# Feed-forward buffers of a whole chunk, two linear steps once per chunk, the first chunk in halves and a new order, in a linear-attention and rational feed-forward kernel

## The chip, the cores and the metric

The kernel runs on one core of one Trainium2 chip. The metric is the device time of one execution in microseconds (us). Five runs of the kernel before gave 249.75, 250.07, 250.63, 252.65 and 254.08 us, a median of 250.63 us.

## What is computed

Two stages follow each other. The first is attention without a softmax: keys and queries (4 batches, 4 heads, 1,088 tokens, 32 numbers each) are turned into 64 features, the outer product of two projections to 8 numbers each. The second is a feed-forward layer whose activation is a quotient of two polynomials. Cut to what matters:

```python
phi(x) = outer(S1 x, S2 x)                      # 8 * 8 = 64 features
kv  = sum over tokens of phi(k) v ; z = sum of phi(k)
x   = (phi(q) kv) / (phi(q) z + 1e-6)           # 4352 tokens x 128
h   = x @ w_in                                  # 128 -> 2048
P   = a0 + a1*h + a2*h^2 + a3*h^3
Q   = 1 + |b0|*|h| + |b1|*h^2
out = (P / (Q + 1e-6)) @ w_out                  # 2048 -> 128
```

## The kernel before, in words

**Tiling.** 4,096 of the 4,352 tokens are worked in eight *chunks* of 512 tokens (two per batch, n = 0 to 7). The 64 last tokens of each batch make a ninth chunk of 256 tokens, the remainder. The 2,048 hidden units are 16 blocks of 128, so the hidden layer of a chunk is a matrix of 128 partitions by 16 x 512 = 8,192 columns. It is worked in *groups* of blocks (`add_group`, L561): the first chunk in groups of 4, 4 and 8 blocks (`FIRST`, L20), each other chunk in two groups of 8 blocks, which is 4,096 columns, and the remainder in 8, 4 and 4 (`LAST`, L21). Groups are numbered g0 to g19 through the whole kernel: g0 to g2 are chunk 0, g3 and g4 chunk 1, g15 and g16 chunk 7, g17 to g19 the remainder.

**A group.** TensorE makes two blocks at a time into PSUM (L572). ScalarE (a few times VectorE) copies them to SBUF as bf16, `hb` (L578, the copy itself in the helper at L184 or L186). Inputs are scaled ahead so that |b0| and |b1| fall out of the formula. VectorE then makes, each one instruction over the whole group:

- `s` = h*h (step `sq`, L582) and `u` = |h| by clearing the sign bit (`ab`, L585)
- `t` = a3*h + a2 (`hi`, L603), `t` = t*s (`cu`, L607), and in place `hb` = a1*h + a0 (`lo`, L610)
- at the end `t` = t*u (`ov`, L621)

Two sums stand between them: `u` = u + s (step `us`) and `t` = t + hb (step `ts`). `add_sum` (L596) gives each of them either to a DMA that accumulates from SBUF into SBUF and is issued by GpSimd (POOL, L594), or to VectorE (L592). ScalarE turns `u` into 1/Q as exp(-ln(..)): `ln` (L614) and `ex` (L618), 4,096 columns at most each. `project` (step `pj`, L629) multiplies `t` by w_out into one PSUM tile for the chunk, which is copied (`eT`) and stored.

**The attention steps.** Per chunk of keys: transposes (L383), projection (L392), copy of one half (`ea`), outer product (`pd`, L403), sum over tokens (L421). Per chunk of queries: transposes (L487), copy (`ev`), expansion by two matmuls (L499), copy of one to `A_sb`, product (`pd`, L506), numerator and denominator (L519), division (`dv`, L526 to L529), transposes of the result (L535) and a copy with a scale to `xT` (`xe`, L540 or L542). With `xT` the matmuls of the hidden layer can begin.

**What sets the order.** Each step is added to a plan with its engine, and `ORDER` (L46) is a list, written out, in which the steps are issued. Each engine carries out its own steps strictly in that order, so a step that waits holds up everything behind it on its engine, DMA issues included. `ENGINE` (L28) names the steps that do not go to their usual engine. `BUFS` (L25) gives the number of buffers: four of one group each for `hb`, `u` and `t`, two for `s`. A tile that takes over a buffer waits until every reader and writer of the tile before it is done. `HOME` (L38) says which PSUM pool small steps use. `fill` steps (L742) are matmuls on zeros; `SKIP` names those left out.

Of the kernel before, what the change touches and what calls it, by code (L numbers as in the profile page):

```python
# [19 lines left out]
FIRST = [4, 4, 8]  # L20
LAST = [8, 4, 4]  # L21
LW = 4096
FILLS = 16

BUFS = dict(xT=3, hb=4, s=2, u=4, t=4, k_sb=2, v=1, q=2, L=1, h_ps=3, out_ps=1, w_ps=1,  # L25
# [3 lines left out]
    "ld.S0": "ACT", "ld.S1": "ACT", "ld.a": "ACT", "ld.b": "ACT", "k00.ea": "DVE", "k01.ea": "DVE", "kr.ev": "DVE",  # L29
    "kr.ea": "DVE", "k0.s0": "DVE", "q1.ev": "DVE", "q2.ev": "DVE", "k20.ea": "DVE", "q5.xe": "DVE", "k30.ea": "DVE",  # L30
    "k31.ea": "DVE", "q7.ev": "DVE", "q8.xe": "DVE", "g1.ts": "DVE", "o0.eT": "DVE", "o1.eT": "DVE", "g7.e4": "DVE",
    "o3.eT": "DVE", "o5.eT": "DVE", "g13.e4": "DVE", "g17.us": "DVE", "g18.ts": "DVE", "o8.eT": "DVE",
}

FOUR = []
SKIP = ["f3"]

HOME = {  # L38
    "k00.T": "h_ps", "k00.ab": "h_ps", "k01.T": "h_ps", "k01.ab": "h_ps", "kv.0": "h_ps", "q0.T": "h_ps",
    "q0.xT": "h_ps", "q1.T": "h_ps", "k11.T": "h_ps", "q2.T": "h_ps", "q2.xT": "h_ps", "q3.T": "h_ps",  # L40
    "q3.xT": "h_ps", "k20.T": "h_ps", "k21.T": "h_ps", "kv.2": "h_ps", "q4.T": "h_ps", "q5.T": "h_ps",
    "q6.T": "h_ps", "q8.T": "h_ps", "q8.xT": "h_ps", "fill.1": "h_ps", "fill.4": "h_ps", "fill.6": "h_ps",
    "fill.9": "h_ps", "fill.11": "h_ps", "fill.12": "h_ps",
# [3 lines left out]
    27, 4, 26, 30, 0, 36, 1, 31, 6, 56, 20, 3, 32, 33, 37, 5, 41, 38, 39, 57, 23, 46, 29, 2, 42, 40, 58, 43, 47, 59,  # L47
    60, 44, 45, 48, 49, 50, 51, 52, 21, 53, 28, 55, 8, 61, 7, 83, 78, 79, 67, 54, 62, 63, 80, 81, 11, 34, 68, 69, 12,
    64, 65, 84, 22, 9, 66, 82, 70, 71, 72, 85, 86, 215, 216, 35, 217, 10, 87, 218, 230, 232, 231, 233, 24, 245, 16,
    220, 219, 115, 247, 116, 246, 248, 222, 224, 234, 235, 237, 223, 221, 226, 73, 74, 75, 249, 250, 238, 239, 240,  # L50
    76, 25, 251, 93, 94, 236, 77, 252, 253, 254, 227, 266, 268, 270, 88, 89, 267, 269, 256, 257, 241, 242, 95, 97,
    272, 271, 225, 14, 228, 273, 229, 243, 104, 105, 90, 258, 244, 96, 91, 92, 274, 277, 285, 98, 130, 201, 117, 99,
    100, 255, 260, 286, 13, 275, 131, 279, 259, 287, 101, 278, 289, 291, 261, 262, 288, 118, 119, 276, 200, 290, 292,
    102, 103, 120, 121, 263, 293, 294, 296, 297, 281, 306, 106, 307, 108, 122, 123, 325, 326, 280, 107, 109, 124,
    264, 298, 282, 283, 308, 309, 310, 312, 152, 295, 311, 313, 300, 265, 110, 111, 112, 327, 284, 153, 329, 314,
    315, 331, 328, 317, 318, 319, 330, 132, 332, 205, 125, 126, 301, 113, 213, 154, 334, 18, 114, 299, 155, 134, 302,
    333, 127, 128, 129, 316, 133, 346, 303, 336, 135, 338, 17, 156, 348, 321, 337, 304, 347, 349, 189, 350, 320, 190,
    365, 203, 157, 351, 322, 323, 352, 15, 136, 366, 141, 158, 137, 353, 138, 142, 335, 340, 305, 324, 367, 368, 355,
    354, 139, 339, 357, 358, 359, 369, 140, 386, 159, 341, 371, 370, 372, 342, 160, 376, 373, 374, 377, 378, 387, 19,
    143, 145, 356, 361, 360, 343, 388, 389, 344, 161, 390, 392, 391, 393, 144, 167, 362, 168, 146, 405, 395, 375,  # L60
    406, 162, 163, 164, 165, 345, 380, 381, 166, 363, 409, 147, 397, 394, 148, 149, 364, 398, 399, 407, 411, 408,
    379, 382, 150, 151, 410, 412, 414, 416, 413, 418, 169, 171, 396, 383, 178, 401, 426, 427, 428, 429, 170, 417,
    172, 179, 384, 445, 402, 430, 431, 432, 173, 446, 174, 181, 400, 433, 403, 175, 435, 404, 434, 415, 420, 437,
    180, 182, 176, 447, 177, 448, 419, 451, 421, 183, 438, 439, 449, 422, 450, 452, 454, 453, 385, 466, 467, 209,
    436, 441, 468, 469, 423, 485, 486, 424, 456, 457, 184, 185, 186, 440, 442, 470, 471, 458, 487, 472, 204, 488,
    489, 473, 443, 474, 475, 444, 477, 478, 455, 460, 191, 193, 425, 459, 187, 188, 479, 491, 490, 492, 192, 461,
    493, 194, 462, 506, 525, 526, 508, 507, 476, 494, 480, 195, 196, 463, 527, 496, 497, 464, 481, 509, 482, 498,
    495, 510, 511, 512, 513, 528, 465, 529, 483, 197, 514, 198, 515, 517, 519, 499, 500, 484, 530, 531, 214, 532,
    501, 548, 546, 533, 207, 534, 547, 516, 535, 502, 549, 553, 518, 536, 538, 520, 561, 562, 563, 537, 564, 551,
    550, 552, 521, 522, 523, 574, 540, 503, 504, 575, 576, 554, 577, 539, 555, 541, 208, 542, 566, 524, 579, 581,  # L70
    580, 568, 567, 569, 557, 558, 565, 570, 571, 505, 199, 578, 556, 559, 582, 543, 211, 206, 212, 544, 545, 210,
    560, 572, 573, 583, 584, 585, 586, 587, 588, 202,
# [40 lines left out]
def kernel(  # L113
# [27 lines left out]
    GW = GF * CW  # L141
# [14 lines left out]
    SHAPES = dict(xT=([128, CW], FP), hb=([128, GW], BF), s=([128, GW], BF), u=([128, GW], BF), t=([128, GW], BF),  # L156
# [199 lines left out]

    W_by = [big.tile([128, NF // 2, d_model], BF, name=f"w_by{i}") for i in range(4)] if FOUR else []
    by_steps = []
    if FOUR:
        ld["wf"] = load("wf", lambda key: starter(key).dma_start(  # L360
            out=new("L", "wf")[:, :NF // 2 * d_model].rearrange("p (n d) -> p n d", d=d_model),
            in_=moe_w_out.rearrange("(fo fi) d -> fi fo d", fi=128)[:, 0:NF // 2, :]), 1740, pk=1024, take=[("L", "wf")], start="SP")

        def by(i):
            o, s = W_by[i].rearrange("p n d -> p (n d)"), T["L", "wf"][:, :NF // 2 * d_model]
            if ENGINE.get(f"c.w{i}", "ACT") == "ACT":
                nc.scalar.mul(o, s, a_sb[:, i:i + 1])
            else:
                nc.vector.tensor_scalar(out=o, in0=s, scalar1=a_sb[:, i:i + 1], scalar2=None, op0=AX.mult)

        for i in range(4):
            alts = dict(ACT=280 + 0.82 * NF // 2 * d_model, DVE=150 + 0.55 * NF // 2 * d_model)
            by_steps.append(plan.add(f"c.w{i}", ENGINE.get(f"c.w{i}", "ACT"), alts[ENGINE.get(f"c.w{i}", "ACT")], lambda i=i: by(i),
                                     after=[ld["wf"], c_inv], give=[("L", "wf")], alts=alts))

# [39 lines left out]
    def add_keys(b):  # L415
# [44 lines left out]
        s = plan.add(f"k{b}.rem", "PE", 540, accumulate_rem, after=[prev, krem_step[0], ld["vr"]])  # L460
# [19 lines left out]
    def add_queries(n, srcs, nt, owners, loads, kv_steps, give=()):  # L480
# [41 lines left out]
        def divide():  # L522
            nb = min(2, nt)
            nd = pair("nd")[:, :nt // nb, :nb * 132].rearrange("p b (g c) -> p b g c", c=D + 1)
            den = new("den", n)[:, :nt // nb, :nb * H]
            nc.vector.tensor_scalar(out=den, in0=nd[:, :, :, D], scalar1=1e-6, scalar2=None, op0=AX.add)  # L526
            nc.vector.reciprocal(out=den, in_=den)
            x = new("x", n)[:, :nt, :].rearrange("p (b i) (h d) -> p b (i h) d", b=nt // nb, h=H)
            nc.vector.tensor_mul(out=x, in0=nd[:, :, :, 0:D],  # L529
                                 in1=den[:, :, :, None].broadcast_to([128, nt // nb, nb * H, D]))  # L530

        def x_transposes():
            p = new(*ps(nm, "xT"))
            for i in range(nt):
                nc.tensor.transpose(p[:, i * 128:(i + 1) * 128], in_=T["x", n][:, i, :], identity=ident)  # L535

        def x_evac():
            o, i = new("xT", n)[:, :W], T[ps(nm, "xT")][:, :W]
            if ENGINE.get(nm + ".xe", "ACT") == "ACT":
                nc.scalar.mul(o, i, sig)  # L540
            else:
                nc.vector.tensor_scalar(out=o, in0=i, scalar1=sig, scalar2=None, op0=AX.mult)  # L542
# [3 lines left out]
        ex = [plan.add(f"{nm}.ex{i}", "PE", 900 * W // 512 + 80, lambda i=i: expand(i), after=[s, c_rep],  # L546
# [5 lines left out]
        for i in range(nt // 2):  # L552
            nd.append(plan.add(f"{nm}.nd{i}", "PE", 520, lambda i=i: num_den(i), after=[s] + nd + kv_steps,
                               take=[("h_ps", nm, "nd")] if i == 0 else [], give=[("q_pT", n)]))
# [4 lines left out]


    def add_group(g, G):  # L561
        W, fis, n = G["W"], G["fis"], G["n"]
        gw = W * len(fis)
        nsub = 1024 // W
        final = fis[-1] == NF - 1
# [219 lines left out]
```

## Time and profile before

| | |
|---|---|
| median of 5 runs | 250.63 us |
| the profiled execution's own time | 249.75 us |
| its span, first to last instruction | 247.9 us |
| VectorE busy | 225.3 us, 91% of the span |
| TensorE busy | 222.8 us, 90% |
| ScalarE busy | 213.9 us, 86% |
| DMA queue of GpSimd (the adds and w_out) | 34.87 MB, 80.0% of 16 engines' span |
| DMA queue of SyncE and ScalarE (loads, stores) | 9.90 MB, 12.9% |
| first instruction of the feed-forward layer on VectorE | starts at 24.77 us |
| last instruction on VectorE | starts at 244.28 us |

The 1.85 us between the time and the span lie around the span. A row of the groups gives busy time, mean duration of one instruction, and the idle time ahead of it on its engine with what ended it. The names PE, DVE, ACT, POOL and SP stand for TensorE, VectorE, ScalarE, GpSimd and SyncE. Where two instructions follow each other without a wait, the second starts before the first has ended in the record, so what one costs its engine is the distance of two starts, which is shorter than its duration.

### The profile page before, as it was taken

How to read it: one execution, taken by the hardware profiler on the slowest of the kernel's cores; microseconds unless marked ns; L12 is line 12 of the kernel's file. 1: busy time of each engine (PE TensorE's matmuls, PEld its weight loads, DVE VectorE, ACT ScalarE, POOL GpSimd, SP SyncE). 2: the span in 40 equal slices, each digit the busy share in tenths (PEclk: the TensorE clock that was granted, in tenths of full speed). 3: DMA queues.
4: the chain of work that ended last, by engine and by line, in shares of the span. 5: the costliest groups of instructions: out<-in, count | busy, mean ns of one | idle time of the engine just before them, and what ended most of it. 6: DMA issues, size and time to landing. Idle time of an engine off the chain costs nothing.

```text
span 247.9 us, 4269 instructions
## 1 busy us (share of the span) xinstructions
PE 222.8 (90%) x1779; PEld 128.6 (52%) x1789; DVE 225.3 (91%) x205; ACT 213.9 (86%) x158; POOL 48.8 (20%) x61
## 2 busy tenths in 40 slices
PE   6999999999999999999999999999998969920783
PEld 2674455654636466563557445546453627710562
DVE  0785999999989989999999999999999999998892
ACT  2335589989989798999999999899989899899991
POOL 4000422132101212112111121212121312113210
PEclk9999999999999999999999999999999999995568
DMA  5895498999998899989999999999999999999982
GB/s 150 271 313 183 71 137 181 167 221 184 185 174 180 147 190 226 233 172 169 171 197 185 180 162 189 194 169 179 200 165 182 178 204 187 178 188 186 201 157 71
DMA packets 23427, 45.11 MB, mean 182 GB/s; under 512 B 5232, under 2 KB 13552, under 8 KB 23408
## 3 DMA queue, kind: packets, MB, share of 16 engines
q0 software_dynamic: 11232, 34.87, 80.0%
q1 hardware_dynamic: 11712, 9.90, 12.9%
q8 instruction: 14, 0.23, 0.4%
q10 hardware_dynamic: 464, 0.08, 0.2%
q14 instruction: 5, 0.04, 0.0%
HBM read 8.79 MB, written 2.23 MB: 44 GB/s over the span
## 4 chain that ended last, share of the span: by engine, by line
PE 37%; DVE 33%; DMA 13%; ACT 9%; issue 7%; SPq 0%; DVEq 0%; ACTq 0%; POOLq 0%
PE h_ps L572 19%; DMA u<-s 7%; DVE s L582 7%; DVE t L621 7%; DVE t L607 5%; ACT u L618 5%; PE h_ps L499 5%; DVE t L603 4%; PE out_ps L629 4%; DVE u L585 4%; DMA t<-hb 4%; DVE hb L610 3%; PE h_ps L421 2%; ACT L L614 2%; ACT hb L184 2%
## 5 line engine op out<-in xcount | busy, mean ns | idle before, releaser
L572 PE MATMUL h_ps<-xT,w_in_sb 128*128 128x512 f32 (+1 forms) x288 | 125.8, 577 | 3.2 <-ACT hb L184 2.6
L572 PEld LDWEIGHTS h_ps<-xT,w_in_sb 128*128 128x128 f32 x288 | 51.7, 190 | 55.4 <-issue 43.1
L184 ACT CAST hb<-h_ps 128x1024 bf16<-128x1024 f32 x66 | 64.6, 1017 | 8.4 <-PE h_ps L572 8.0
L614 ACT ACTIVATE L<-u,one_ap,lsc 128x4096 f32<-128x4096 bf16 (+2 forms) x20 | 65.9, 3294 | 5.4 <-DMA u<-s 5.1
L618 ACT ACTIVATE u<-L 128x4096 bf16<-128x4096 f32 (+2 forms) x20 | 62.3, 3114 | 0.2
L629 PE MATMUL out_ps<-w_out,t 128*128 128x128 bf16 x544 | 36.6, 230 | 14.7 <-DVE t L621 14.7
L594 POOL DMA_DIRECT2D u<-s x19 | 24.1, 1269 | 118.0 <-DVE u L585 54.6
L629 PEld LDWEIGHTS <-t 128*128 128x128 bf16 x544 | 33.9, 104 | 22.4 <-DVE t L621 19.2
L621 DVE TENSOR_TENSOR t<-t,u 128x4096 bf16<-128x4096 bf16 (+2 forms) x20 | 39.2, 1967 | 3.2 <-ACT u L618 1.7
L582 DVE TENSOR_TENSOR s<-hb 128x4096 bf16<-128x4096 bf16 (+2 forms) x20 | 39.2, 1963 | 1.5 <-ACT hb L184 1.5
L607 DVE TENSOR_TENSOR t<-t,s 128x4096 bf16<-128x4096 bf16 (+2 forms) x20 | 39.3, 1967 | 0.3
L594 POOL DMA_DIRECT2D t<-hb x18 | 21.6, 1200 | 72.4 <-issue 20.2
L610 DVE TENSOR_SCALAR hb<-hb,a_sb 128x4096 bf16<-128x4096 bf16 (+2 forms) x20 | 23.8, 1188 | 0.2
L603 DVE TENSOR_SCALAR t<-hb,a_sb 128x4096 bf16<-128x4096 bf16 (+2 forms) x20 | 23.6, 1182 | 0.0
L585 DVE TENSOR_SCALAR u<-hb 128x4096 int16<-128x4096 int16 (+2 forms) x20 | 22.3, 1114 | 0.1
L499 PE MATMUL h_ps<-qT,Srep 64*128 64x512 f32 (+1 forms) x72 | 19.5, 617 | 0.4 <-ACT hb L184 0.4
L506 DVE TENSOR_TENSOR q_pT<-A_sb,h_ps 128x1024 f32<-128x1024 f32 (+1 forms) x9 | 10.4, 1156 | 2.6 <-ACT A_sb L184 1.4
L519 PEld LDWEIGHTS h_ps<-kv,q_pT 128*64 128x64 f32 (+1 forms) x288 | 8.7, 134 | 5.1 <-issue 2.8
L519 PE MATMUL h_ps<-kv,q_pT 128*64 128x66 f32 (+1 forms) x288 | 10.1, 225 | 0.0
L184 ACT COPY A_sb<-h_ps 128x1024 f32<-128x1024 f32 (+1 forms) x9 | 8.7, 964 | 0.8 <-PE h_ps L499 0.8
L499 PEld LDWEIGHTS h_ps<-qT,Srep 64*128 64x128 f32 x72 | 5.4, 184 | 6.9 <-ACT hb L184 2.1
L184 ACT COPY kT<-h_ps 128x512 f32<-128x512 f32 x5 | 2.9, 585 | 5.3 <-PE h_ps L383 4.8
(89 smaller groups left out, 134.5 us busy)
## 6 DMA issues: line engine op xcount, KB each, us to landing
u<-s POOLq DMA_DIRECT2D x15, 1024.0 KB, 8.5
t<-hb POOLq DMA_DIRECT2D x15, 1024.0 KB, 9.5
k_sb<-in_k_dram SPq DMA_DIRECT2D x4, 512.0 KB, 4.7
q<-in_q_dram SPq DMA_DIRECT2D x8, 256.0 KB, 4.9
v<-in_v_dram SPq DMA_DIRECT2D x4, 512.0 KB, 7.9
out_dram<-oT SPq DMA_DIRECT2D x8, 256.0 KB, 6.4
w_in_sb<-in_moe_w_in_dram SPq DMA_DIRECT2D x2, 512.0 KB, 5.5
u<-s POOLq DMA_DIRECT2D x2, 512.0 KB, 7.4
```

What stands on the lines that cost most here:

```text
L184: nc.scalar.copy(out=out, in_=in_)
L499: nc.tensor.matmul(pair(i)[:, g, :W], lhsT=Srep[i][rows].rearrange("p g f -> p (g f)"), rhs=T["qT", n][rows, :W], start=True, stop=True)
L572: nc.tensor.matmul(p[:, i * W:(i + 1) * W], lhsT=w_in_sb[:, fi * 128:(fi + 1) * 128], rhs=T["xT", n][:, :W], start=True, stop=True)
L582: nc.vector.tensor_mul(out=new("s", g)[:, :gw], in0=h, in1=h)
L585: nc.vector.tensor_scalar(out=new("u", g)[:, :gw].bitcast(mybir.dt.int16), in0=T["hb", g][:, :gw].bitcast(mybir.dt.int16), scalar1=0x7FFF, ...
L594: nc.gpsimd.dma_start(out=d, in_=s, accum_op=AX.add, max_dma_last_dim=4096)
L603: nc.vector.tensor_scalar(out=new("t", g)[:, :gw], in0=T["hb", g][:, :gw], scalar1=a_sb[:, 3:4], scalar2=a_sb[:, 2:3], op0=AX.mult, op1=AX ...
L607: nc.vector.tensor_mul(out=T["t", g][:, :gw], in0=T["t", g][:, :gw], in1=T["s", g][:, :gw])
L614: nc.scalar.activation(out=new("L", g, l0)[:, :lw], in_=T["u", g][:, l0:l0 + lw], func=ACT.Ln, bias=one_ap, scale=lsc)
L618: nc.scalar.activation(out=T["u", g][:, l0:l0 + lw], in_=T["L", g, l0][:, :lw], func=ACT.Exp, scale=-1.0)
L621: nc.vector.tensor_mul(out=T["t", g][:, :gw], in0=T["t", g][:, :gw], in1=T["u", g][:, :gw])
L629: nc.tensor.matmul(T["out_ps", n][:, j * 128:(j + 1) * 128], lhsT=T["t", g][:, c:c + 128], rhs=W_out[:, fis[i], :], start=fis[i] == 0 and ...
```

## The change

- `hb`, `s`, `u` and `t` become tiles of a whole chunk (8,192 columns), and `BUFS` has half as many of them: two `hb`, one `s`, two `u`, two `t`. The bytes stay the same.
- In chunks 1 to 7 the steps `hi` and `lo` (`WIDE`) are one instruction over 8,192 columns instead of two over 4,096. The other steps stay in groups.
- The first chunk has groups of 2, 2, 4 and 8 blocks. Its division, transposes and scaled copy are done in two halves of the tokens (`SPLIT`), and its first two blocks are multiplied in two halves of the columns.
- The groups after the first chunk have their number raised by one: g4 and g5 are chunk 1, g16 and g17 chunk 7, g18 to g20 the remainder.
- `ENGINE` changes. Sums on VectorE were g1.ts, g17.us and g18.ts (2,048, 2,048 and 1,024 columns). They are now g2.us (2,048), g4.us, g6.ts, g15.ts, g16.ts (4,096 each), g19.ts and g20.us (1,024 each). Copies move between ScalarE and VectorE both ways.
- `ORDER`, `HOME` and `SKIP` are new lists; five fill steps are left out where it was one. The unused path `FOUR` is removed.
- In the order of loads on SP, the first queries now stand ahead of the first keys, and two more transfers (queries of chunk 1, keys of batch 1) ahead of the first values.

```diff
-FIRST = [4, 4, 8]
+FIRST = [2, 2, 4, 8]
+WIDE = ["hi", "lo"]
+SPLIT = [0]
-BUFS = dict(xT=3, hb=4, s=2, u=4, t=4, k_sb=2, v=1, q=2, L=1, h_ps=3, out_ps=1, w_ps=1,
+BUFS = dict(xT=3, hb=2, s=1, u=2, t=2, k_sb=2, v=1, q=2, L=1, h_ps=3, out_ps=1, w_ps=1,
 ENGINE = {
-    "ld.S0": "ACT", "ld.S1": "ACT", "ld.a": "ACT", "ld.b": "ACT", "k00.ea": "DVE", "k01.ea": "DVE", "kr.ev": "DVE",
-    "kr.ea": "DVE", "k0.s0": "DVE", "q1.ev": "DVE", "q2.ev": "DVE", "k20.ea": "DVE", "q5.xe": "DVE", "k30.ea": "DVE",
-    "k31.ea": "DVE", "q7.ev": "DVE", "q8.xe": "DVE", "g1.ts": "DVE", "o0.eT": "DVE", "o1.eT": "DVE", "g7.e4": "DVE",
-    "o3.eT": "DVE", "o5.eT": "DVE", "g13.e4": "DVE", "g17.us": "DVE", "g18.ts": "DVE", "o8.eT": "DVE",
+    "ld.S0": "ACT", "ld.S1": "ACT", "ld.a": "ACT", "ld.b": "ACT", "k00.ea": "DVE", "k01.ea": "DVE", "k0.s0": "DVE",
+    "q1.xe": "DVE", "k10.ea": "DVE", "k11.ea": "DVE", "k1.s0": "DVE", "k1.s1": "DVE", "q3.ev": "DVE", "k2.s1": "DVE",
+    "k3.s0": "DVE", "q6.xe": "DVE", "q7.xe": "DVE", "g2.us": "DVE", "g4.e2": "DVE", "g4.us": "DVE", "g6.ts": "DVE",
+    "g13.e0": "DVE", "g15.ts": "DVE", "g16.ts": "DVE", "g20.us": "DVE", "g19.ts": "DVE", "o8.eT": "DVE",
 }
...
-    SHAPES = dict(xT=([128, CW], FP), hb=([128, GW], BF), s=([128, GW], BF), u=([128, GW], BF), t=([128, GW], BF),
+    SHAPES = dict(xT=([128, CW], FP), hb=([128, FW], BF), s=([128, FW], BF), u=([128, FW], BF), t=([128, FW], BF),
...
+        if n in SPLIT:
+            out = []
+            for i in range(2):
+                s = plan.add(f"{nm}.dv{i}", "DVE", 830, lambda i=i: divide(i), after=[nd[i]] + out[-1:], give=[("h_ps", nm, "nd"), ("den", n)],
+                             take=[("x", n), ("den", n)] if i == 0 else [])
+                s = plan.add(f"{nm}.xt{i}", "PE", 250, lambda i=i: x_transposes(i), after=[s], take=[ps(nm, "xT", i)],
+                             flex=[ps(nm, "xT", i)], give=[("x", n)])
+                out.append(add_copy(f"{nm}.xe{i}", lambda i=i: x_evac(i), W // 2, ptr=1, after=[s, c_b] + out[-1:],
+                                    take=[("xT", n)] if i == 0 else [], give=[ps(nm, "xT", i)]))
+            return out
...
+        def units(op):
+            return whole if op in WIDE and 0 < n < len(chunks) else parts
+
+        def at(buf, f0, f1):
+            return T[buf, n][:, f0 * W:f1 * W]
...
+        def wide(op, fn, buf, cost, after, give=()):
+
+            made[op] = []
+            for nm, f0, f1 in units(op):
+                gw = (f1 - f0) * W
+
+                def go(f0=f0, f1=f1, first=not made[op]):
+                    if buf and first:
+                        new(buf, n)
+                    fn(f0, f1)
+
+                deps = [x for a in after for x in (over(made[a], f0, f1) if isinstance(a, str) else [a])]
+                made[op].append((f0, f1, plan.add(f"{nm}.{op}", "DVE", cost(gw), go, after=deps + [x[2] for x in made[op][:1]],
+                                                  take=[(buf, n)] if buf and not made[op] else [], give=give)))
...
+        wide("sq", d_sq, "s", tt, ["e"])
+        wide("ab", d_ab, "u", ts, ["e"])
+        sum_of("us", "u", "s", ["sq", "ab"], [("s", n)])
+        wide("hi", d_hi, "t", tp, ["e", c_inv])
+        wide("cu", d_cu, None, tt, ["hi", "sq"], give=[("s", n)])
+        wide("lo", d_lo, None, tp, ["hi", "ab", "sq"])
+        sum_of("ts", "t", "hb", ["cu", "lo"], [("hb", n)])
```

## The prediction, made before the changed kernel was run

> **What bounds the kernel now.** First the page's busy times, then the windows by stage, the waits of VectorE, the groups with shapes kept apart, and the order of time on VectorE. Busy times (us, share of the span, instructions):
>
> ```profile
> PE 222.8 (90%) x1779; PEld 128.6 (52%) x1789; DVE 225.3 (91%) x205; ACT 213.9 (86%) x158; POOL 48.8 (20%) x61
> ```
>
> No engine stands out. By windows (length, busy of PE, PEld, DVE, ACT, POOL, then clock, DMA share, GB/s):
>
> ```profile
> 0.00:24.77 24.77, 22.89 (x250) 13.59 (x251) 13.88 (x34) 9.69 (x15) 2.68 (x23) 1.00 0.77 229
> ...
> 40.00:100.00 60.00, 59.02 (x525) 33.66 (x528) 56.66 (x44) 55.25 (x47) 12.02 (x9) 1.00 0.97 185
> 100.00:160.00 60.00, 58.80 (x478) 32.72 (x478) 58.94 (x47) 58.01 (x40) 11.38 (x10) 1.00 0.98 186
> 160.00:220.00 60.00, 55.22 (x351) 31.87 (x353) 58.83 (x43) 57.05 (x36) 13.31 (x11) 1.00 1.00 182
> 220.00:240.00 20.00, 7.81 (x66) 6.84 (x68) 18.49 (x20) 19.54 (x10) 5.12 (x6) 0.57 1.00 185
> 240.00:247.90 7.90, 3.92 (x39) 2.37 (x38) 3.39 (x5) 2.78 (x3) 0.06 (x1) 0.91 0.36 85
> ```
>
> From 100 to 220 us VectorE is busy 117.8 of 120 (98%), ScalarE 115.1 (96%) and the DMA engines 98 to 100%: three resources end together. VectorE's idle time is the account I work with: 10.9 us before its first feed-forward instruction at 24.77, 7.3 between 24.77 and 240 (0.2 of it up to 40; 3.3, 1.1, 1.2 and 1.5 in the four windows after), 4.5 after 240. What it waits for (total, times, longest):
>
> ```profile
> DVE t L621 <- ACT u L618: 1.7, 4, 0.5
> DVE s L582 <- ACT hb L184: 1.5, 1, 1.5
> DVE q_pT L506 <- ACT A_sb L184: 1.4, 1, 1.4
> DVE den L526 <- PE h_ps L519: 1.2, 3, 0.7
> DVE t L621 <- DMA t<-hb: 1.2, 2, 0.7
> ```
>
> Only 1.2 us of this is put down to a DMA. Prices, from the order of time (start, duration): a product of 4,096 columns costs 2.20 us from start to start, `hi` or `lo` 1.26, `ab` 1.13; of 1,024 columns 0.61 and 0.46.
>
> ```profile
> 127.74 2.29 DVE L582 TENSOR_TENSOR s<-hb 128x4096 bf16<-128x4096 bf16 x1
> 129.94 2.29 DVE L621 TENSOR_TENSOR t<-t,u 128x4096 bf16<-128x4096 bf16 x1
> 132.14 1.34 DVE L603 TENSOR_SCALAR t<-hb,a_sb 128x4096 bf16<-128x4096 bf16 x1
> 133.40 1.22 DVE L585 TENSOR_SCALAR u<-hb 128x4096 int16<-128x4096 int16 x1
> 134.53 0.17 DVE L526 TENSOR_SCALAR den<-h_ps 128x16 f32<-128x16 f32 x1
> ...
> 237.52 0.55 DVE L610 TENSOR_SCALAR hb<-hb,a_sb 128x1024 bf16<-128x1024 bf16 x1
> 237.98 0.69 DVE L607 TENSOR_TENSOR t<-t,s 128x1024 bf16<-128x1024 bf16 x1
> 238.59 0.54 DVE L610 TENSOR_SCALAR hb<-hb,a_sb 128x1024 bf16<-128x1024 bf16 x1
> 239.04 0.68 DVE L607 TENSOR_TENSOR t<-t,s 128x1024 bf16<-128x1024 bf16 x1
> ```
>
> **What the Trainium skill says.** "VectorE: DVE Perf Modes", section "The TRN2 errata — SBUF-src ops pay a fixed extra latency per instruction": a large tile pays the fixed cost once; its measured fixed term is about 150 cycles at 0.96 GHz, 0.16 us. The trace agrees: rows of `lo` take 1,350 ns at 4,096 columns and 808 at 2,048, so 542 ns per 2,048 and 0.27 us fixed by duration, or 1.26 - 1.08 = 0.18 from start to start. "DMA: Bandwidth & Descriptors", section "Issuing engines are not separate DMA queues": all transfers share the same 16 engines, so an add taken off relieves the loads too. The shares of 0.97 to 1.00 fit. "SBUF — State Buffer", section "Who interferes with whom": VectorE in a two-port mode, which `tensor_scalar` can enter, and GpSimd lock each other out for a whole instruction. The trace has one such case: an `ab` of 2,048 columns took 1.78 us (the others 0.69) while GpSimd issued w_out.
>
> **The change part by part.** VectorE's work, start to start:
>
> - Adds. g2.us replaces g1.ts at equal size. Four of 4,096 columns and two of 1,024 come, one of 2,048 (1.14) and one of 1,024 go: 4 x 2.20 + 2 x 0.61 - 1.75 = +8.3 us.
> - `hi` and `lo` merged in seven chunks, 14 pairs: 2 x 1.26 - (1.26 + 1.08) = 0.18 each, -2.5 us. No row shows 8,192 columns. Bounds: no saving (0), or the whole fixed duration, 14 x 0.27 = 3.8 us.
> - Copies. Off VectorE go four output copies (4 x 0.60), four of transposes (3 x 0.60 + 0.34), four `ea` (0.9), two `xe` (0.66 + 0.39): 6.5. To it come three `xe` (2.0), eight small copies of kv (8 x 0.19), two `ea` (0.5), one `ev` (0.6): 4.6. Net -1.9. The two copies of `hb` stay two.
> - First chunk: one more group means three products (0.09 fixed each), two `hi`/`lo` (0.18) and one `ab` (0.06), 0.7 us; the second half of the division, three more instructions, 0.5. +1.2.
>
> Sum +5.1 us of work on an engine that is busy 98% of the steady part. It has to come out of idle time.
>
> Start. Before, VectorE first waits 1.4 us for `A_sb` (ahead of L506) and then 1.5 us until two pairs of blocks are multiplied (1.77 us a pair) and copied (1.0). After, one pair is enough: -1.77. The expansion of chunk 1's queries stands earlier on TensorE, so the wait for `A_sb` goes; the transposes of chunk 2's queries (0.55) stand ahead of the hidden matmuls, the halved division gives about 0.9 back. I place the first feed-forward instruction at 22.65, 2.1 us earlier. A pair of blocks costs VectorE 0.46 + 0.33 + 0.61 + 0.61 + 0.46 = 2.5 us, more than TensorE's 1.77, so it isn't starved behind that. Unknown: the first values are issued behind 0.75 MB more. At the 300 to 430 GB/s of these microseconds that is 1.7 to 2.5 us, and their sum over tokens is in the chain of waits (11.17 us). TensorE has 1 us more of transposes to do ahead of it; I take 0 and keep 0 to +2. Behind that sum wait all of TensorE's queue and so the first chunk.
>
> DMA: 15,360 columns fewer, 3.9 MB. GpSimd's queue took 198.3 us for 34.87 MB, 5.7 us per MB: 22 us less. ScalarE gets about 1.5 us more (net of copies, one more pair of `ln` and `ex`); it was idle 13.8 us between 24.77 and 240. TensorE's halves cost below 0.5 us; it waits 12.2 us for `t` near the end.
>
> Waits between 24.77 and 240. I follow the new order with these durations and a landing time of 9 us. VectorE waits some 0.5 us for the eighth copy of chunk 0's last group, 0.5 for that group's `ex`, 0.4 for g4's add by DMA. Then what it needs is there first: the four adds of 4,096 columns put 2.2 us in the place of a landing of 8.5 to 9.5 (g4.us, g6.ts, and near the end g15.ts and g16.ts, where it now waits 0.7 and 0.6 for t<-hb). The merged `hi` waits for all eight copies of a chunk, but stands behind `sq`, `ab` or `ov` that cover that. I add 1.0 us for small waits on TensorE that a reckoning by hand misses: 2.4 instead of 7.3, -4.9. The last 4.5 us stay: `pj`, the output copy and the store are the same.
>
> Sum: 247.9 + 5.1 - 2.1 - 4.9 = 246.0 us of span, 1.9 less. The profiled execution's own time of 249.75 would become 247.9; the median, 0.9 above it, 248.7 us.
>
> **Rivals.**
>
> 1. VectorE's waits vanish (below 1 us), since only it is left at the bound. At none: 247.9 + 5.1 - 2.1 - 7.3 = 243.6 of span, 246.3 us. For it: ScalarE and TensorE run some microseconds ahead in my reckoning and DMA has 22 us to spare. Against: most waits named above are for TensorE and ScalarE, whose loads do not fall.
> 2. The waits stay. Taken at its word, the list frees only the 1.2 us put down to DMA: 247.9 + 5.1 - 2.1 - 1.2 = 249.7, 252.4 us: adds were moved off an engine that nobody waited for. Against: a full DMA queue also delays `ln`, which waited 5.1 us for u<-s, and so `ov`.
> 3. Slower: the single `s`. The first `sq` of a chunk must wait until the last u<-s of the chunk before has landed. In the new order VectorE has 9.3 us of other work between them from chunk 0 to 1, 11.3 from 1 to 2, 11.6 from 4 to 5, 12.4 from 5 to 6, over 14 elsewhere. u<-s lands in 8.5 us (median, longest 10.9). At a landing of L the first three lose 3L - 32.2 us: it takes 4.4 us over my forecast to be 1% slower, so it decides from 12.2 us. Merged `hi` and `lo` can hold GpSimd's issue up to 2.3 us, which speaks for it; the 22 us less of traffic against.
> 4. The merging does nothing: +2.5, 251.2 us.
>
> **How the numbers follow.** A measurement of this kernel can tell about 1% from no change, here 248.1 to 253.1 us. My forecast with 1.5 to 5 us of waits (247.8 to 251.3) has 0.48; of this 0.14 lies below 248.1. Rival 1 has 0.28, rivals 2 and 4 together 0.12, rival 3 or late first values beyond 253.1 have 0.12. Faster 0.14 + 0.28 = 0.42, within 1% 0.34 + 0.12 = 0.46, slower 0.12. The range runs from 245.0 (rival 1 and the merging's upper bound) to 252.8.
>
> **What would show it.** Right: first feed-forward instruction near 22.7 us; 8,192-column rows near 2.4 us; VectorE's busy time near 230 us; its idle time between 24.77 and 240 near 2.4; a DMA share near 0.9. Wrong: L597 waiting for u<-s (rival 3), waits of VectorE on TensorE above 4 us (rival 2), a first sum over tokens after 13 us.

## The result, and the profile after

The changed kernel takes 249.9 us (median of 43 runs) where the kernel before, run beside it, takes 251.02 us (80 runs). The ratio is 0.9957, interval 0.9943 to 0.9970: faster by 0.43%, within the 1% that the forecast called no change. The forecast was 1.9 us less, the measurement 1.1. Two later repeats gave 0.9963 (0.9944 to 0.9983) and 0.9989 (0.9965 to 1.0013).

The profiled execution takes 249.59 us, its span is 247.8 us, against 247.9 before. Its busy times:

```profile
PE 223.2 (90%) x1782; PEld 130.1 (53%) x1785; DVE 229.1 (92%) x204; ACT 215.5 (87%) x161; POOL 49.3 (20%) x59
```

VectorE has 3.8 us more work; the others are nearly where they were. The windows by stage, cut at VectorE's first feed-forward instruction (length, busy of PE, PEld, DVE, ACT, POOL, then clock, DMA share, GB/s):

```profile
0.00:25.44 25.44, 22.56 (x254) 14.38 (x255) 13.78 (x35) 10.27 (x17) 2.67 (x23) 1.00 0.72 223
25.44:40.00 14.56, 14.56 (x75) 6.86 (x74) 14.38 (x22) 9.90 (x10) 5.27 (x6) 1.00 0.70 91
40.00:100.00 60.00, 60.00 (x510) 34.38 (x508) 58.60 (x45) 56.88 (x45) 11.39 (x9) 1.00 0.88 167
100.00:160.00 60.00, 60.00 (x466) 33.15 (x465) 59.56 (x43) 59.20 (x43) 14.57 (x10) 1.00 0.91 169
160.00:220.00 60.00, 51.43 (x367) 30.26 (x369) 59.51 (x37) 57.60 (x38) 10.69 (x8) 1.00 0.93 173
220.00:240.00 20.00, 10.88 (x81) 8.70 (x81) 19.93 (x22) 19.84 (x11) 4.70 (x5) 0.75 0.82 154
240.00:247.80 7.80, 3.78 (x41) 2.38 (x39) 3.29 (x5) 1.81 (x3) 0.00 (x0) 0.94 0.30 75
```

From 40 to 240 us VectorE idles 2.4 us (1.4, 0.4, 0.5 and 0.1) where it idled 7.1, and the DMA share has come down from 0.97 to 1.00 to some 0.9. But the first feed-forward instruction starts at 25.44 instead of 24.77, and the idle time ahead of it is 25.44 - 13.78 = 11.7 instead of 10.9 us. The list of VectorE's waits says on what:

```profile
DVE sT L328 <- PE h_ps L324: 4.3, 1, 4.3
DVE b_abs L345 <- DMA b_sb<-in_moe_b_dram: 2.0, 1, 2.0
DVE k_p_rem L387 <- ACT a_t L187: 1.6, 1, 1.6
...
DVE t L627 <- ACT u L624: 0.4, 1, 0.4
DVE t L627 <- DMA t<-hb: 0.4, 1, 0.4
```

The waits of the feed-forward layer have shrunk to entries of 0.4 us. A new one stands second: 2.0 us for `b_sb`, a load of 1 KB. (The third, for a copy on ScalarE, is new too, but it holds nothing up: the product behind it is done at 13.33 us, and TensorE takes it at 13.76, right after the work ahead of it.) The order of time shows what is behind the wait for `b_sb`. In the kernel before, the load went out at once, and its use had no wait:

```profile
1.73 0.37 ACTq L241 DMA_DIRECT2D b_sb<-in_moe_b_dram  x1
...
14.66 0.16 DVE L342 TENSOR_SCALAR b_abs<-b_sb 128x2 int32<-128x2 int32 x1
```

In the changed kernel, on ScalarE and its queue:

```profile
11.91 0.59 ACT L187 COPY kT<-h_ps 128x512 f32<-128x512 f32 x1 [1.66 <-PE h_ps L367]
11.95 0.36 ACTq L244 DMA_DIRECT2D a_sb<-in_moe_a_dram  x1
12.36 0.44 ACTq L244 DMA_DIRECT2D b_sb<-in_moe_b_dram  x1
```

then on VectorE:

```profile
14.49 0.46 DVE L454 COPY kv<-w_ps 64x66 f32<-64x66 f32 x2
16.97 0.17 DVE L345 TENSOR_SCALAR b_abs<-b_sb 128x2 int32<-128x2 int32 x1 [2.02 <-DMA b_sb<-in_moe_b_dram]
...
17.77 0.17 DVE L514 TENSOR_SCALAR den<-h_ps 128x8 f32<-128x8 f32 x1
...
25.44 0.55 DVE L604 TENSOR_SCALAR t<-hb,a_sb 128x1024 bf16<-128x1024 bf16 x1 [0.28 <-ACT hb L187]
```

The new order puts both loads of coefficients on ScalarE's queue behind seven copies of queries and keys; before, `b_sb` was issued at 1.73 us and `a_sb` at 6.68, behind two copies. The copy at 11.91 had waited 1.66 us for TensorE, so `b_sb` goes out at 12.36. It is on its way 4.6 us, and the step that makes the scale from it stands ahead of the first division on VectorE. The chain of waits runs through it:

```profile
12.36 4.59 DMA b_sb<-in_moe_b_dram
...
18.77 0.41 PE h_ps L528 x2
```

### The profile page after: what moved, and what is told of

It reads as the page before. It is cut to its first block, busy times and chain, and to the rows that moved or that the text cites. A ratio compares the mean times of both kernels' runs of the same rounds, so it can differ in the third digit from the quotient of the medians.

```text
span 247.8 us, 4266 instructions
## 1 busy us (share of the span) xinstructions
PE 223.2 (90%) x1782; PEld 130.1 (53%) x1785; DVE 229.1 (92%) x204; ACT 215.5 (87%) x161; POOL 49.3 (20%) x59
## 3 DMA queue, kind: packets, MB, share of 16 engines
q1 hardware_dynamic: 11712, 9.90, 12.4%
## 4 chain that ended last, share of the span: by engine, by line
PE 59%; DVE 20%; DMA 10%; issue 5%; ACT 4%; SPq 0%; POOLq 0%; ACTq 0%; DVEq 0%
PE h_ps L588 34%; PE out_ps L634 7%; PE h_ps L483 6%; DVE t L627 5%; DMA u<-s 5%; PE h_ps L503 3%; DVE t L608 3%; DVE t L604 2%; PE h_ps L405 2%; DVE hb L611 2%; DVE s L597 2%; DMA t<-hb 2%; DVE u L600 2%; DMA b_sb<-in_moe_b_dram 2%; DMA k_sb<-in_k_dram 2%
## 5 line engine op out<-in xcount | busy, mean ns | idle before, releaser
L588 PEld LDWEIGHTS h_ps<-xT,w_in_sb 128*128 128x128 f32 x292 | 52.7, 190 | 55.6 <-issue 43.5
L187 ACT CAST hb<-h_ps 128x1024 bf16<-128x1024 f32 x66 | 65.9, 1019 | 9.9 <-PE h_ps L588 9.4
L618 POOL DMA_DIRECT2D u<-s x18 | 25.9, 1437 | 115.0 <-DVE s L597 60.8
L618 POOL DMA_DIRECT2D t<-hb x17 | 20.0, 1260 | 74.0 <-DVE t L608 43.6
L611 DVE TENSOR_SCALAR hb<-hb,a_sb 128x8192 bf16<-128x8192 bf16 (+3 forms) x14 | 23.2, 1656 | 0.1
L604 DVE TENSOR_SCALAR t<-hb,a_sb 128x8192 bf16<-128x8192 bf16 (+3 forms) x14 | 22.0, 1568 | 0.3 <-ACT hb L187 0.3
L600 DVE TENSOR_SCALAR u<-hb 128x4096 int16<-128x4096 int16 (+2 forms) x21 | 21.3, 1016 | 0.0
L616 DVE TENSOR_TENSOR t<-t,hb 128x4096 bf16<-128x4096 bf16 (+1 forms) x4 | 7.5, 1885 | 0.0
```

The source lines that it names most:

```text
L187: nc.scalar.copy(out=out, in_=in_)
L588: nc.tensor.matmul(p[:, i * W + c0:i * W + c1], lhsT=w_in_sb[:, fi * 128:(fi + 1) * 128], rhs=T["xT", n][:, c0:c1], start=True, stop=True)
L604: nc.vector.tensor_scalar(out=at("t", f0, f1), in0=at("hb", f0, f1), scalar1=a_sb[:, 3:4], scalar2=a_sb[:, 2:3], op0=AX.mult, op1=AX.add)
L611: nc.vector.tensor_scalar(out=at("hb", f0, f1), in0=at("hb", f0, f1), scalar1=a_sb[:, 1:2], scalar2=a_sb[:, 0:1], op0=AX.mult, op1=AX.add)
L618: nc.gpsimd.dma_start(out=at(dst, f0, f1), in_=at(src, f0, f1), accum_op=AX.add, max_dma_last_dim=4096)
```

## The experiments

All ratios are to the kernel before, run beside the edited one. Experiments 2, 3, 6, 8, 11 and 13 have six runs each, 9 has 11, 12 has 13, the others have 22. `ORDER` holds numbers; the diffs write the names of the steps. Where profiles are compared, the time of the first feed-forward instruction and VectorE's idle time are set out as in the forecast; a single profile's span scatters by a microsecond, from TensorE's start above all, so verdicts are by the ratios.

**1. The late load, taken early.**

```diff
-  k0.s0, ld.b, c.b, k0.s1, ...      and ld.a ahead of q1.ex0
+  ld.S1, q0.tr, ld.S0, ld.b, ld.a, c.sT, ...
```

> The changed kernel with one edit: the two small loads of the polynomial coefficients (a_sb, b_sb), which stand behind the copies of keys on ScalarE's queue and land at 14 to 17 us, are issued there right behind the load of S, as the first work. Theory (the start term failed because VectorE's scale step waits 2.0 us for b_sb, and with it the first division, its transposes and the first hidden matmuls): b_sb lands before 8 us, the wait is gone, the first feed-forward instruction starts at 23.4 to 23.8 us instead of 25.4, and the time falls by 1.6 to 2.0 us, a ratio to the kernel before of 0.988 to 0.990. Rival (another chain in the start, or the steady part, takes up what is won): the ratio stays at 0.9957 within 0.2%.

Ratio 0.9982 (0.9954 to 1.0010): the wait for `b_sb` is gone from the list, and nothing is won. The profile shows another loss in its place, ahead of the first keys' transposes on TensorE:

```profile
5.57 0.28 PE L323 MATMUL h_ps<-ident,SR 16*128 16x16 f32 x1
7.08 1.12 PE L366 MATMUL h_ps<-ident,k_sb 128*128 128x128 f32 x4 [1.22 <-DMA k_sb<-in_k_dram]
```

The same step starts at 5.53 in the changed kernel, with a wait of 0.2 us at most. Besides, TensorE takes 1.5 us longer here from these transposes to the sum over tokens. The copy of the first sums, at 14.49 there, is at 17.55 here; from it to the first feed-forward instruction it takes 26.91 - 17.55 = 9.4 us instead of 25.44 - 14.49 = 10.9. So the local part of the theory held and its forecast of the time missed.

**2. The kernel before, with its loads late.**

```diff
-  ld.kr, ld.b, c.s12, ...   c.ones, ld.a, k01.ev, ...
+  c.clear, k0.s1, ld.b, ld.a, ld.k1, ...
```

> The kernel before with one edit: its two small loads of coefficients are moved on ScalarE's queue behind the copy of the first sums of keys (13.75 us there), much where the changed kernel has them. b_sb then lands near 18.3 us, 3.7 to 4 us after VectorE would use it. Theory (a late start on VectorE passes to the end one to one): 3 to 3.7 us slower, ratio 1.012 to 1.015. Rival (a slip in the start is taken up by the 7.3 us of waits in the middle): ratio 1.000 to 1.004.

Ratio 1.0198 (1.0146 to 1.0249), 5 us. Its first feed-forward instruction starts at 29.55 instead of 24.77, 4.8 us later: the wait for `b_sb` is 3.1, VectorE then waits 2.3 us for a product of queries where it waited 1.4, and TensorE's sum over tokens had started 0.5 later to begin with. In this execution TensorE also ran at a granted clock of 0.61 from 19.8 to 24.2 us, after a wait of 2.4; its expansions there take 1.43 and 1.96 us where they take 1.13 in the kernel before. I had mis-sized the slip, but it passes to the end in full: the waits in the middle take up nothing of it (9.2 us in this execution instead of 7.3).

**3. The four adds given back to the DMA.**

```diff
-    ... "g4.us": "DVE", "g6.ts": "DVE", "g15.ts": "DVE", "g16.ts": "DVE", ...
```

> The changed kernel with the four sums of 4,096 columns (g4.us, g6.ts, g15.ts, g16.ts) given back to the accumulating DMA, all else as it is. VectorE's work falls by 4 x 2.20 = 8.8 us, the DMA queue gets 4 MB and about 22 us of transfer. Theory (these adds are what took the waits of the middle away, at a price on VectorE that is just about paid back): VectorE's idle time between its first feed-forward instruction and 240 us rises from 2.6 to 8 to 12 us, the DMA share from 0.9 to about 1.0, and the time stays within 1% of the changed kernel, ratio to the kernel before 0.990 to 1.003. Rival (the waits fell because of the order alone, and VectorE's work alone sets the time): 6 to 8 us faster, ratio 0.965 to 0.972. Other rival (without them the DMA is the bound): slower by 4 us or more, ratio above 1.012.

Ratio 1.0534 (1.0483 to 1.0585): my theory missed, and the time is that of the other rival. VectorE has 8.5 us less work (220.6), and its idle time between the first feed-forward instruction and the last 7.9 us is 26.0 us instead of 2.6:

```profile
DVE t L627 <- DMA t<-hb: 10.4, 4, 5.7
DVE q_pT L490 <- PE h_ps L483: 5.3, 2, 4.5
DVE den L514 <- PE h_ps L503: 4.9, 3, 2.1
```

The DMA share is 0.98 from 100 to 220 us. But the other rival's reason, that the DMA engines are the bound, does not hold as it stands: between VectorE's first feed-forward instruction and the last 7.9 us their share is 0.92, where the kernel before, with about the same traffic, had 0.98 and took 13 us less. A landing of 9.1 us stands where the order left room for 2.2; experiment 11 shows one more way in which the adds cost time.

**4. Without merging.**

```diff
-WIDE = ["hi", "lo"]
+WIDE = []
```

> The changed kernel with the steps hi and lo in two instructions of 4,096 columns, one right behind the other at the place of the wide one, instead of one of 8,192. Theory (each merged pair saves the fixed part, 0.18 us from start to start, on an engine that is busy 98%): 14 x 0.18 = 2.5 us slower, ratio to the kernel before 1.005 to 1.007. Rival (the merging does nothing, since the fixed part is hidden or the waits take it up): ratio stays at 0.9957 within 0.2%.

Ratio 1.0053 (1.0027 to 1.0078), 0.6 to 1.0% above the changed kernel's three ratios, 1.6 to 2.4 us. In the changed kernel the wide steps take 2.44 and 2.33 us from start to start:

```profile
65.69 2.41 DVE L604 TENSOR_SCALAR t<-hb,a_sb 128x8192 bf16<-128x8192 bf16 x1
68.13 2.41 DVE L611 TENSOR_SCALAR hb<-hb,a_sb 128x8192 bf16<-128x8192 bf16 x1
70.46 2.29 DVE L608 TENSOR_TENSOR t<-t,s 128x4096 bf16<-128x4096 bf16 x1
```

and here the same two pairs 2.62 and 2.51 (each row is two instructions):

```profile
68.15 2.71 DVE L604 TENSOR_SCALAR t<-hb,a_sb 128x4096 bf16<-128x4096 bf16 x2
70.77 2.58 DVE L611 TENSOR_SCALAR hb<-hb,a_sb 128x4096 bf16<-128x4096 bf16 x2
73.28 2.28 DVE L608 TENSOR_TENSOR t<-t,s 128x4096 bf16<-128x4096 bf16 x1
```

0.18 us a pair, 14 pairs: the forecast's 2.5 us. VectorE's busy time is 2.8 us longer (231.8).

**5. The changed kernel again**, as the yardstick for 6 to 8.

> The changed kernel without any edit, as the yardstick on the chip of the three runs beside it. Expected: 0.9957 of the kernel before, within 0.3%, first feed-forward instruction of VectorE near 25.4 us.

Ratio 0.9963. The first feed-forward instruction is at 26.10, since TensorE was slower in its first microseconds (below).

**6. The late load, taken in the middle.**

```diff
-  k0.s0, ld.b, c.b, k0.s1, ...
+  k01.pr, k00.ev, ld.b, c.rep, ...
```

> The changed kernel with one load moved, b_sb, on ScalarE's queue from behind the last copies of keys to behind the second one of the first chunk (8.4 us), where the first keys have landed and the queue is free: it lands near 13 us, ahead of its use at 15, and takes nothing from the loads of the first 7 us as the very early place did. Theory (the start term failed by the 2.0 us wait for b_sb): the wait is gone, the first division starts at 16.2 us instead of 17.8, the first feed-forward instruction at 23.8 to 24.2 instead of 25.4, and the time falls by 1.2 to 1.6 us, ratio to the kernel before 0.989 to 0.991. Rival (the start is bound by another chain, or what is won in the start comes back as waits in the middle): less than 0.4 us, ratio 0.994 to 0.997.

Ratio 0.9904 (0.9869 to 0.9939), 248.7 us beside 250.0 of the changed kernel: 1.3 less. The profiled execution started as slowly as that of experiment 5 (copies of the first sums at 15.87 and 15.89 us on ScalarE), so the two compare: the first feed-forward instruction is at 24.66 instead of 26.10, 1.44 us earlier.

```profile
15.68 0.15 DVE L344 TENSOR_SCALAR b_abs<-b_sb 128x2 int32<-128x2 int32 x1
...
16.99 0.17 DVE L513 TENSOR_SCALAR den<-h_ps 128x8 f32<-128x8 f32 x1 [0.55 <-PE h_ps L502]
```

No wait is left at `b_abs`, and 0.55 us at the division, for TensorE, where 2.0 had been.

**7. Without the halves.**

```diff
-SPLIT = [0]
+SPLIT = []
```

> The changed kernel with the first chunk's division, transposes, scaled copy and first pair of blocks whole instead of in two halves of the tokens (each at the place of the second half). Theory (halving wins little here, because the second half follows the first after 2.2 us with an outer product between them): first feed-forward instruction 0.3 to 1.0 us later, time 0 to 1 us longer, ratio to the kernel before 0.996 to 1.000. Rival (the halves are worth what the forecast gave them and hide part of the wait for b_sb): 1.5 us or more longer, ratio above 1.001.

Ratio 0.9963 (0.9942 to 0.9985), the same as with them. The first feed-forward instruction is at 24.82 us, 0.6 earlier than in the changed kernel, where theory and rival alike had expected a loss. TensorE's order gives a reason why the halves win nothing. In the changed kernel:

```profile
21.38 0.44 PE L528 MATMUL w_ps<-ident,x 128*128 128x128 f32 x2
21.75 0.69 PE L376 MATMUL h_ps<-S,kT 128*64 128x64 f32 x16
22.36 3.71 PE L588 MATMUL h_ps<-xT,w_in_sb 128*128 128x256 f32 x12
```

The hidden matmuls of the first half stand behind the second half's transposes (21.38) and a projection of keys. `xT` of the first half was ready at 19.7; the first half's matmuls start 2.7 us later, right ahead of the second's.

**8. The kernel before with the four adds on VectorE.**

```diff
+    "g3.us": "DVE", "g5.ts": "DVE", "g14.ts": "DVE", "g15.ts": "DVE",
```

> The kernel before with one edit: the four sums of 4,096 columns that the change gives to VectorE (one of chunk 1, one of chunk 2, two near the end) are done by VectorE there too, at the places at which their DMAs were issued. VectorE gets 8.8 us more work, the DMA queue 22 us less. Theory (moving adds off the full DMA queue takes waits away only together with an order made for it): VectorE's waits between its first feed-forward instruction and 240 us fall from 7.3 to 3 to 5, the work counts in full, and the time is 4 to 7 us longer, ratio 1.016 to 1.028. Rival (the adds alone buy the waits back, the order is not needed): ratio 0.995 to 1.008.

Ratio 1.0234 (1.0194 to 1.0274): the work counts in full, 8.3 us of busy time, and its waits in the middle fall only from 7.3 to 4.8. With experiment 3 this makes a table of four:

| ratio to before | four adds by DMA | four adds on VectorE |
|---|---|---|
| kernel before | 1 | 1.0234 |
| the rest of the change | 1.0534 | 0.9957 |

Neither part pays alone. The lower row is more than the new order: buffers, merged steps, halves and copies are in it too. Without merging (experiment 4) and without the halves (7) VectorE's idle time in the middle stays at 1.8 and 3.1 us, so these two are not what lets the adds pay. That leaves the order, the buffers and the copies, which no run takes apart.

**9. Middle load and no halves.**

> Both edits on the changed kernel: b_sb loaded in the middle place (as in the run that moves this load alone) and the first chunk's division, transposes, scaled copy and first blocks whole. Theory (the halves win nothing, with or without the late load, because TensorE's queue puts the first half's hidden matmuls behind the second half's transposes): within 0.3% of the run with the load moved alone, ratio to the kernel before 0.987 to 0.992. Rival (the halves were only hidden behind the wait for b_sb and count once it is gone): 1 us or more slower than that run, ratio above 0.994.

Ratio 0.9923 (0.9883 to 0.9962). That agrees with the theory, but its interval reaches past the rival's 0.994, so the time alone doesn't settle the halves' worth with the load in the middle place. The profiles speak for the theory: from the start of the sum over tokens to the first hidden matmul TensorE takes 9.06 us here and 9.02 with the halves (experiment 13). Its profile has a wait of 1.21 us for `k_sb`, although the load stands in the middle place:

```profile
6.91 0.66 PE L366 MATMUL h_ps<-ident,k_sb 128*128 128x128 f32 x4 [1.21 <-DMA k_sb<-in_k_dram]
```

So the late first keys of experiment 1 are not proof that the early loads delayed them.

**10. `b_sb` alone early.**

> The changed kernel with b_sb alone as the first load behind S on ScalarE's queue (1.7 us), where the kernel before has it; a_sb stays late. Theory (in the run with both loads early, their some 290 small packets stood in the DMA queues ahead of the first keys, which landed 1.5 us later, so TensorE waited 1.2 us and ran slower for longer): with one load the first keys come at most half as late, the wait of TensorE for k_sb is 0 to 0.6 us, and part of the gain of the middle place shows, ratio 0.990 to 0.996. Rival (the early place is harmless and the other run met only a slow start of TensorE): as the middle place, 0.989 to 0.992, with no wait for k_sb.

Ratio 0.9969 (0.9944 to 0.9993). No wait for `k_sb` in its profile, but 0.71 us for the next queries; the wait for `b_sb` is gone, and the first feed-forward instruction is at 24.87. The ratio lies above both expectations, though its interval overlaps the theory's. Early places win little or nothing, and why is not settled; in the profiles of both the sum over tokens starts late (see the table further down).

**11. Only the two adds of chunks 1 and 2 given back.**

> The changed kernel with only the two sums of chunks 1 and 2 (g4.us, g6.ts) given back to the accumulating DMA; the two near the end stay on VectorE. VectorE's work falls by 4.4 us. Theory (each add given back exposes the part of its landing of 9 us for which the order has no cover, wherever it stands): about half of the loss of the run with all four, 6 to 8 us slower than the changed kernel, ratio to the kernel before 1.020 to 1.030. Rival (only the two near the end matter, where the two longest waits for t<-hb stand, 5.7 and 4.1 us): ratio 0.990 to 1.005.

Ratio 1.0158 (1.0112 to 1.0204), 1.7 to 2.0% above the changed kernel's three ratios: 4.2 to 5.0 us, less than the theory's 6 to 8 and about a third of the loss of experiment 3. The rival is out. VectorE's idle time in the middle is 12.3 us for 4.0 us less work, most of it (7.7) between 40 and 100 us. The longest of these waits is 3.4 us for TensorE, and TensorE in turn had waited for a load of queries:

```profile
67.96 0.63 PE L471 MATMUL w_ps<-ident,q 128*128 128x128 f32 x4 [3.58 <-DMA q<-in_q_dram]
```

Three loads of queries issued from 55 us on land after 12.4 us (median) instead of 8.1 in the changed kernel, and the DMA share from 54 to 68 us is 1.01 instead of 0.71. Experiment 3 has the same wait of TensorE (3.2 us). So an add by DMA costs more than its own landing: it also delays the loads that run beside it.

**12 to 14. The wait taken away without moving a load.** The steps that use `b_sb` are put one place later on VectorE; beside it experiment 6 and the changed kernel once more.

```diff
-  k0.s0, ld.b, c.b, k0.s1, ... q0.dv0, k11.tr, ...
+  k0.s0, ld.b, k0.s1, ... q0.dv0, c.b, k11.tr, ...
```

> The changed kernel with no load moved: instead VectorE's four small steps that use b_sb stand one place later, behind the first half of the first division, which does not need them. The loads are issued exactly as in the changed kernel. Theory (the wait for b_sb in front of the first division is the failed step of the start): the first division starts at 16.1 us instead of 17.8, the wait left for b_sb is 0 to 0.3 us, the first feed-forward instruction starts at 23.9 to 24.5 us when TensorE starts as in the profile of the changed kernel, and the time falls by 1.0 to 1.5 us against the changed kernel beside it. Rival (it was the moved load that helped, or only its chip and few runs): less than 0.4 us.

> The kernel with b_sb loaded in the middle place once more, beside the changed kernel and the one with the later use, since it had only six runs and the start scatters by about 1 us from run to run (first keys landing late, TensorE at first slower) in all kernels of this case. Theory: 1.0 to 1.5 us under the changed kernel beside it, as the first time, and within 0.3% of the kernel with the later use. Rival: no better than the changed kernel (within 0.2%).

> The changed kernel once more, unedited, as the yardstick of the two runs beside it: ratio to the kernel before 0.994 to 0.998.

Ratios: later use 0.9924 (0.9895 to 0.9954), 249.27 us; middle load 0.9886 (0.9843 to 0.9929), 248.82; changed kernel 0.9989, 250.4. So 1.1 and 1.6 us less than the changed kernel beside them. In the kernel with the later use the loads go out as in the changed kernel (`b_sb` at 12.49), and

```profile
16.30 0.17 DVE L513 TENSOR_SCALAR den<-h_ps 128x8 f32<-128x8 f32 x1 [1.22 <-PE h_ps L502]
...
17.08 0.16 DVE L344 TENSOR_SCALAR b_abs<-b_sb 128x2 int32<-128x2 int32 x1
```

the division starts 1.5 us earlier and `b_sb` is there when it is wanted, with no wait. The first feed-forward instruction is at 24.18 us, with the middle load at 23.78. Taking the wait away gives 1.1 to 1.6 us, whether by the middle place or by the later use. The early places (experiments 1 and 10) take it away too and give little or nothing. The kernel with the middle load has the lowest ratios of all here, 0.9904 and 0.9886 in two sets of runs, about 1% under the kernel before.

## Why the prediction was right or wrong

The forecast's sum against the profile of the changed kernel, in us:

| term | forecast | measured |
|---|---|---|
| VectorE's work | +5.1 | +3.8 |
| idle before its first feed-forward instruction | -2.1 | +0.8 |
| idle from there to 240 us | -4.9 | -4.7 |
| tail | 0 | 0 |
| span | -1.9 | -0.1 |

By these profiles the span hardly moves, while the medians differ by 1.1 us. The profiled execution of the kernel before is one of its fastest, 1.3 us under the median of 251.02; that of the changed kernel is 0.3 under its own. The difference of 1.0 is what the profiles leave out.

**The step that failed is the start**: "I place the first feed-forward instruction at 22.65, 2.1 us earlier". It came at 25.44, 2.8 us after that. TensorE's chain shows where. In the kernel before:

```profile
11.00 2.04 PE L421 MATMUL h_ps<-v,k_p 128*64 128x64 f32 x64
...
19.99 8.85 PE L572 MATMUL h_ps<-xT,w_in_sb 128*128 128x512 f32 x20
```

and in the changed kernel, with the hidden matmuls from 22.36 on:

```profile
11.16 0.66 PE L367 MATMUL h_ps<-ident,k_sb 128*128 128x128 f32 x4
11.74 2.09 PE L405 MATMUL w_ps<-v,k_p 128*64 128x64 f32 x64
```

The profiled executions, cut at the same two points (us; more than one number for more than one execution, the added ones by the numbers of their experiments):

| kernel | sum over tokens starts | from there to the first hidden matmul | to VectorE's first feed-forward instruction |
|---|---|---|---|
| before (and 8) | 11.00, 11.53 | 8.99, 8.93 | 13.77, 13.72 |
| changed (and 3, 5, 11, 14) | 11.74, 11.70, 12.57, 11.65, 12.15 | 10.62, 10.52, 10.45, 10.36, 10.58 | 13.70, 13.60, 13.53, 13.44, 13.66 |
| loads early (1, 10) | 14.81, 12.76 | 9.02, 9.03 | 12.10, 12.11 |
| load in the middle (6, 13) | 12.56, 11.68 | 9.02, 9.02 | 12.10, 12.10 |
| used later (12) | 11.88 | 9.23 | 12.30 |
| no halves (7) | 11.70 | 10.05 | 13.12 |
| no halves, load in the middle (9) | 13.32 | 9.06 | 12.13 |

Experiments 2 and 4 are left out: their profiled executions have a stretch of low granted clock here (last section).

The 2.8 us come apart as follows:

- 1.4 to 1.7 us is the wait for `b_sb` (1.44 between experiments 5 and 6; 25.44 - 23.78 = 1.66 between the changed kernel and experiment 13). The forecast followed the loads that the diff says were moved, those on SP. The two that the new `ORDER` moves on ScalarE's queue, behind seven copies, it did not look at, so its sum has no term for this wait. The table shows it between the sum and the hidden matmuls wherever the step that needs `b_sb` waits for it, and nowhere else. That it costs time is shown by experiments 6, 12 and 13, and 2 shows that such a slip passes to the end in full. With the early places the stretch is as short, but in their profiled executions the sum starts late; whether the moved loads do that is open, since experiment 9, with the load in the middle, starts it at 13.32.
- 0.7 us is the start of the sum of values and keys, 11.74 on TensorE instead of 11.00, with the transposes of later keys ahead of it (11.16, 0.58 us). The forecast named these transposes ("1 us more") and the late values, and put both at nothing: "I take 0 and keep 0 to +2". TensorE did not wait for the values. No run moved the transposes, so this part is read from the trace and not tested.
- 0.4 us is "the halved division gives about 0.9 back", less the 0.55 that the forecast set against it for transposes. Neither shows: without the wait the stretch from the sum to the hidden matmuls is 9.02 us with the halves, 9.06 without them, and 8.99 in the kernel before. (The forecast's 2.1 is 1.77 + 0.9 - 0.55. The 1.4 us wait ahead of the product of queries, of which it says that it goes, is not in this sum, and 0.7 us of it is still there.)
- The other half of this step, one pair of blocks instead of two, was right: from the first hidden matmul to the first feed-forward instruction it takes 25.44 - 22.36 = 3.1 us instead of 24.77 - 19.99 = 4.8, so 1.7, forecast 1.77.

**The waits in the middle** were right in sum, 2.6 us against 2.4 forecast, and in the main in their cause. The four adds take away waits for t<-hb, for queries that the DMA brings late, and what hangs on them, but they pay only with the rest of the change (experiments 3, 8, 11). Rival 2, that adds were moved off an engine for which nobody waited, is refuted for the changed kernel; for the kernel before, experiment 8 comes near it: 8.3 us of work buy back 2.5 us of waits. Rival 1, no waits at all, did not come.

**The work** was 1.3 us too high, and 1.1 of it is the merging. Counted over the whole trace, from each instruction's start to its end or to the next start if that comes first, the adds cost 8.3 us more (forecast 8.3), the copies 1.7 less (1.9), and the additions of the first chunk come to 1.1 (1.2). But the `hi` and `lo` of chunks 1 to 7 cost 32.7 us instead of 36.3, so 3.6 less where the forecast had 2.5. It priced an unmerged one at 1.26 us, read where the next step starts before it has ended. In the order of before many have no such overlap:

```profile
41.04 1.34 DVE L603 TENSOR_SCALAR t<-hb,a_sb 128x4096 bf16<-128x4096 bf16 x1
42.41 2.29 DVE L607 TENSOR_TENSOR t<-t,s 128x4096 bf16<-128x4096 bf16 x1
```

Their mean is 1.30. In experiment 4, which has the rest of the change, the unmerged ones cost 35.5 us, 2.8 more than the merged: so 2.8 is the merging itself, and 0.8 comes with the rest of the change. The 1.78 us that one `ab` took beside the issue of w_out by GpSimd is only moved: in the changed kernel a `lo` of 1,024 columns takes 1.60 us beside the same issue, where others take 0.55 to 0.63.

**Rival 3**, the single `s`: it is never waited for in the changed kernel. u<-s lands in 9.6 us (median), against the 12.2 from which it would have decided. **Rival 4**, merging without effect, is refuted by experiment 4.

That the total came out as near as it did is in part luck: 1.3 us less work stood against 2.9 us more idle time at the start. With the wait for `b_sb` taken away the forecast's 1.9 us is reached or passed: experiments 12, 6 and 13 lie 1.9, 2.4 and 2.9 us under the kernel before by their ratios.

## What to carry to other kernels

When a change rewrites an order, list for every queue what now stands ahead of each small load, not only for the queues that the change names: a load of 1 KB issued behind a copy that waits cost 1.1 to 1.6 us here, as much as the whole change won. The earliest place was not the best one for it. An add that is moved from a transfer to an engine has one price together with the rest of a change that was made around it; here either alone cost 2.3% and 5.3%. And before halving a step, look where what follows the first half stands in its engine's queue: here it stood behind the second half, and halving won nothing.

## What the runs showed of the hardware

- TensorE starts at different paces in executions of the same code. The first four transposes of queries, at 4.6 us, took 0.70 us in one execution of the changed kernel and 1.06 in another (experiment 14); the like ones later take 0.60 to 0.66. In slow starts the first sums lie up to 0.8 us later (12.57 in experiment 5 against 11.74). With the loads in the same places, TensorE waited 1.2 us for the first keys in one execution (experiment 9) and 0.2 at most in another (experiment 13).
- TensorE's granted clock fell to 0.61 and 0.66 for some 4 to 5 us in two profiled executions (experiment 2 from 19.8 us, after TensorE had waited 2.4 us; experiment 4 from 19.7, after 1.6). In the changed kernel it stayed at 1.00 after a wait of 1.6, so the wait alone doesn't decide it.
- The load of 1 KB took 4.0 to 5.3 us from issue to landing when issued at about 2 us or from 12 to 14 us, nearly as long as the loads of 512 KB at the start of the kernel before (medians 4.7 to 6.6 us). Issued at 9 to 10 us (experiments 6, 9 and 13) it took 2.5.
- An add of 1 MB by accumulating DMA lands in 9.6 us (u<-s) and 8.6 (t<-hb) in the changed kernel, at a DMA share of 0.88 between VectorE's first feed-forward instruction and 240 us, against 8.5 and 9.5 before at 0.98, and in 8.2 and 8.9 in experiment 8 at 0.85. Less traffic made a single one little or no quicker.
- Loads of 256 KB of queries beside such adds took 8.1 us (median of three) at a DMA share of 0.71 and 12.4 at 1.01 (changed kernel and experiment 11, 54 to 68 us).
